# First q and k rows in 1 KB pieces on two partition halves, cast by head pairs, in a fused window attention and mixture of experts

## The chip, the cores and the metric

The kernel runs on one core of a Trainium2 chip. The time is device time of one execution in microseconds (us), as the median of several executions. A core has five engines that matter here. TensorE multiplies matrices and is written PE in the profile; loading its weights, which runs beside the multiplying, is written PEld. VectorE is DVE, ScalarE is ACT, GpSimd is POOL, and SyncE is SP. SP and ACT start transfers on hardware queues (q1 and q10 in the profile), POOL on a software queue (q0). [...]

## The reference: what is computed

Two stages, in float32. First comes attention with a window and sinks, over 4 batches, 8 heads, 768 positions and 64 dimensions per head:

```
scores = q @ k.T / sqrt(D)
keep   = (key position < 4) | ((0 <= query - key) & (query - key < 128))
a      = softmax(where(keep, scores, -1e9));  out = a @ v
```

The heads of a position are then laid side by side, which gives x with 3072 rows (tokens) of 512. Second comes a mixture of four experts with all of them used:

```
p   = domain_probs / (domain_probs.sum(-1) + 1e-9)
out = sum over e of  p[:, e] * (relu(x @ w1[e]) @ w2[e])      # w1: 512x1024, w2: 1024x512
```

## The kernel before

**Tiling.** Tokens are handled in groups of 256 (`G`): three groups in each of the four batches. Within a group, attention goes by head pairs (`hp`, four of them), since two heads of 64 dimensions fill the 128 partitions. For each pair and group it computes scores (line 676), their exponential on ACT (line 702), a mask, the product with v (lines 736 and 743), and the division by the sum (lines 770 to 782). The result is turned so that the 512 features lie on partitions (`xT`). The mixture then takes a group and an expert as a unit: first product and relu (line 1051 in the plain form, lines 1138 to 1206 in a Strassen form with seven products instead of eight), second product (line 1388 plain, line 1312 Strassen).

**Order of the work.** All engines get their instructions in a fixed order, written by a planner that runs in Python while the kernel is built. It keeps a clock for each engine and queue (`t`), estimates when each transfer has landed (`lands`, line 183, with the constants `t["sw"]`, `ROW` and `BACKLOG`), and picks the next piece of work for PE by readiness and rank (`LOW_PRODUCT`, `DUE`, `OPEN` and so on). Work for DVE and ACT waits in a list and is given out by due time (`later`, `flush`). `WIDE` is how many units of the first product may be open at once, `MIX` how many units of batch 0 may be left when batch 1 begins, `PAIR` the first batch in which two head pairs' scores may be issued together, `BACKLOG` an allowance on the landing of everything behind the first weights. When the planner sees PE with nothing ready it inserts products on zeros (`idle_products`, line 546); nine of these stand at the very start. The planner's estimates set only the order: at run time an engine waits at an instruction until its inputs are there, and all that stands behind it waits too.

**The beginning.** `load_first` (line 254) brings the first 256 positions of q and k of batch 0 as float32. They come in two halves of four heads, q from SP's queue and k from ACT's queue. Each partition holds two neighbouring positions of a head, so a contiguous piece is 2 x 64 x 4 bytes = 512 bytes, and each of the four transfers covers 128 partitions. `cast_first` (line 275) makes bf16 of them, q on DVE and k on ACT, one instruction for each half; a head pair can be turned only when both casts of its half are done. `transposes` (line 556) turns a pair with four PE transposes, two of q into one PSUM tile and two of k into another, and DVE copies q and ACT copies k into `qkT`. All other rows of batch 0 come on the software queue (`load_nat`, line 230, in 256-byte pieces), in this order: v blocks 0 and 1, q and k blocks 2 and 3, v blocks 2 and 3, the two halves of expert 0's w1, its w2, q and k blocks 4 and 5, and then the other experts. Later batches' q and k are turned by transposing transfers from SP (`turn_nat`, line 241).

**Constants and sinks.** Before the first cast, DVE makes the identity in bf16, a selector `sel2`, and a triangular mask by a scan over the identity (line 499). The identity comes from two selections on POOL (line 478). SP loads the value rows of the four sink positions, for all batches, with eight small transfers (line 473). When attention of batch 0 is done, SP stores the gates (`gates_by_row`, line 432) and the loads of batch 1 are put on the list.

Of the kernel before, what the change touches and what calls it, by code (L numbers as in the profile page):

```python
# [9 lines left out]
ALU = mybir.AluOpType  # L10
AX = mybir.AxisListType
# [5 lines left out]
def kernel(  # L17
# [44 lines left out]
    MIX = 5  # L62
    SHARE_OF = (1.034, 1.037, 1.072)
    LEAD = (1.026, 0.9853)
    DUE = 1.356
    LOW_PRODUCT = 2.147
    LOW_SECOND = 2.509
    HIGH_PRODUCT = -1
    EARLY = 0.1973
    MASK_SLACK = 200.0  # L70
    GATE = 2639.0
    GATE0 = 6000.0
    FORM = 1000.0
    TOKEN = 4559.0
    MARGIN = 2117.0
    HOLD = 0
    FULL = 8
    STEP0 = 0.2923
    READY = 40
    WIDE = 3  # L80
    OPEN = 2.551
    ONACT = 1
    ONE = 2
    PAIR = 0
    BEHIND = 2351.0
# [12 lines left out]
    t = {"pe": 1200.0, "act": 0.0, "dve": 0.0, "pool": 1280.0, "sp": 800.0, "sw": 4800.0, "hw": 0.0}  # L98
    ring, whole = [0.0] * 6, [False] * 6
    WARM = 6600.0  # L100
    FLIP, LATE = 103.6, 500.0
# [79 lines left out]
    ROW = {64: 12.8, 128: 22.6, 512: 79.8, 1024: 156.2}  # L181

    def lands(key, rows, cols, *deps):
        issued = pool(0, *deps, fixed=880)
        at = max(t["sw"], issued + 1500)
        t["sw"] = at + rows * ROW[cols] / 16
        landed[key] = t["sw"] + 900 + (BACKLOG if key[0] == "w1" or backed else 0.0)
        if key[0] == "w1":
            backed.append(key)
        moved.append([key, at, t["sw"], ROW[cols]])  # L190

    moved, backed = [], []
    BACKLOG = 1300.0
# [59 lines left out]

    def load_first():

        raw = {name: mo.tile([P, 2, 4, 2 * D], FP32, name=f"{name}raw", tag=f"wide{i}", bufs=1) for i, name in enumerate("qk")}
        for half in range(2):
            hs = slice(4 * half, 4 * half + 4)
            for name, src in (("q", q), ("k", k)):
                x = raw[name][:, half]  # L260
                (nc.sync if name == "q" else nc.scalar).dma_start(
                    out=x, in_=src[0, hs, 0:G, :].rearrange("h (p t) d -> p h (t d)", t=2),
                )
                nat[0, half, name, "raw"] = x
            landed["first", half] = ((4870.0, 5180.0), (7550.0, 7350.0))[half]
            t["sp"] += 530
# [4 lines left out]
    first = {name: sb.tile([P, 2, H, D], BF16, name="qkn", tag="qkn", bufs=NQB) for name in "qk"}  # L271
    qkn_free[-2:] = [1e12] * 2
    cast_at = {}

    def cast_first(half):
        hs = slice(4 * half, 4 * half + 4)

        def cast(at):
            cast_at[half] = at

        part = join(2, cast)
        for i, name in enumerate("qk"):
            def run(engine, i=i, name=name):
                copy(
                    engine, first[name][:, :, hs, :],
                    nat[0, half, name, "raw"].rearrange("p h (t d) -> p t h d", t=2),
                )
                part(clock(engine, 512))
            later(("dve", "act")[i], landed["first", half][i], 0, run)
# [137 lines left out]
    identf = scratch[:, 9 * P:10 * P]  # L427
    nc.sync.dma_start(out=dp, in_=moe_domain_probs.rearrange("(tb p) e -> tb p e", p=P))
# [42 lines left out]
    for h in range(H):  # L471
        r = 32 * (h // 2) + NSINK * (h % 2)
        nc.sync.dma_start(
            out=vsf[r:r + NSINK, :, 0:D], in_=v[:, h, 0:NSINK, :].rearrange("b j d -> j b d"),
        )
    ident = consts.tile([P, P], BF16, name="ident")
    for sgn in (1, -1):
        nc.gpsimd.affine_select(
            out=identf, in_=identf, compare_op=ALU.is_ge, fill=0.0,
            base=0, pattern=[[sgn, P]], channel_multiplier=-sgn,  # L480
        )
        pool(0, fixed=320)
# [3 lines left out]
    for tb in (2, 3):  # L486
# [6 lines left out]

    nc.vector.tensor_copy(out=ident, in_=identf)
    nc.vector.reduce_sum(
        out=sel2, in_=identf.rearrange("p (h x j) -> p h x j", h=NHP, j=NSINK)[:, :, 0:2], axis=AX.X,
    )
    own = lent[:, 4 * P:5 * P]
    nc.vector.tensor_tensor_scan(own, ident, ident, 0.0, ALU.add, ALU.max)
# [15 lines left out]
    def make_mask(i):  # L515
        def run(engine):
            x = (mask0, mask1)[i]
            nc.vector.tensor_scalar(out=x, in0=low[i], scalar1=1 / LOW, scalar2=1.0, op0=ALU.mult, op1=ALU.add)
            dve(4 * P)
            made.append(i)  # L520
        later("dve", 9500.0, 5000, run)
# [3 lines left out]
    t["dve"] = t["act"] = 4600.0  # L525
    cast_first(0)
    flush(4700.0)
    for x in vx:
        nc.vector.memset(x[:, :, D:DX], 1.0)
    t["dve"] += 240.0  # L530
# [25 lines left out]
    def transposes(b, g, hp):  # L556

        if b not in qkT:
            qkT[b] = sb.tile([P, 2, NHP, S], BF16, name="qkT", tag="qkT", bufs=1)
        ready = max(cast_at[hp // 2] if (b, g) == (0, 0) else rows_at(b, g), free_at(2 if (b, g) == (0, 0) else 1))  # L560
        slots, trs = [], []
        for i in range(2 if (b, g) == (0, 0) else 1):
            slots.append(pick())
            trs.append(bank(slots[i], [P, 2, 2, P], BF16, "tr"))
            ring[slots[i]] = 1e12
        hs = slice(2 * hp, 2 * hp + 2)
        for i in range(2):
            for tt in range(2):
                rows = first["qk"[i]][:, tt, hs] if (b, g) == (0, 0) else nat[b, 2 * g + tt][:, i, hs]
                nc.tensor.transpose(trs[i if (b, g) == (0, 0) else 0][:, i, tt], rows, ident)  # L570
        done = pe(4 * P, ready, n=4)
        dst = qkT[b][:, :, hp, g * G:(g + 1) * G]

        def copied(at):
            for slot in slots:
                take(slot, at)
            turned_at[b, g, hp] = at

        if (b, g) == (0, 0):
            part = join(2, copied)  # L580
            for i, engine in enumerate(("dve", "act")):
                def run(engine, i=i):
                    copy(engine, dst[:, i].rearrange("c (p t) -> c p t", t=2), trs[i][:, i].rearrange("c t p -> c p t"))
                    part(clock(engine, 2 * P))
                later(engine, done, 0, run)
        else:
            def run(engine):
                copy(engine, dst, trs[0].rearrange("c i t p -> c i (t p)"))
                copied(clock(engine, 4 * P))
            later("any", done, 300, run)  # L590
        if hp == NHP - 1:
            for _ in range(2):
                qkn_free.remove(1e12)
                qkn_free.append(done)
            qkn_free.sort()
# [221 lines left out]
    class Attention:  # L817
# [21 lines left out]
        def flip_ready(self):  # L839
            _, b, g, hp = self.flips[0]  # L840
            rows = cast_at.get(hp // 2, 1e12) if (b, g) == (0, 0) else rows_at(b, g)
            return max(rows, free_at(2 if (b, g) == (0, 0) else 1), scored_at.get(b - 1, 0.0))
# [68 lines left out]
    NH = 6  # L911
# [534 lines left out]
    while mix.more() or att.more():  # L1446
# [5 lines left out]
        if not att.more() and not loaded:  # L1452
            loaded = 1
            gates_by_row()
            turns += [(1, tb) for tb in range(NQB)]
# [102 lines left out]
```

## Time and profile before

| | |
|---|---|
| median of 3 runs | 362.27 us (361.88 to 362.48) |
| the profiled execution | 362.99 us, of which its span is 361.2 us |
| PE busy in the span | 351.7 us (97%) |
| DVE / ACT / POOL busy | 296.4 / 164.9 / 70.4 us |
| granted TensorE clock | full in every slice |
| software queue q0 | 17.31 MB in 77520 packets |
| hardware queue q1 | 18.75 MB in 38668 packets |
| hardware queue q10 (ACT's, used for the first k alone) | 0.52 MB in 1056 packets |

The span runs from the first instruction to the last, and the profiled execution's own time is 1.8 us longer. The page splits the span into 40 slices and gives the busy share of each engine in tenths. The chain of waits is followed back from the last instruction: at each step to what released it. A timeline row gives start, duration, engine, line, operation, output, inputs and count; in brackets stands how long the engine was idle before it and what ended that. In the table of stretches the columns after the stretch are its length and the busy time of PE, PEld, DVE, ACT and POOL with the number of instructions, the granted clock, the busy share of the 16 DMA engines (over 1 where several transfers are under way in each) and GB/s. Packets of the software queue are counted by the bytes that they write, so one of 128 bytes has read 256.

### The profile page before, as it was taken

Reading aid. Unit: us, or ns where it says so; the run is one execution under the profiler, and the core shown is the slowest. Engines: PE = TensorE matmul, PEld = TensorE weight load, DVE = VectorE, ACT = ScalarE, POOL = GpSimd, SP = SyncE. Lnnn points to the kernel's source line nnn. Section 1 sums busy time; section 2 is a strip of 40 time slices with the busy share of each in tenths; the row PEclk is TensorE's granted clock in tenths of the full one; section 3 lists DMA queues with packets and bytes.
Section 4 is the critical chain, followed back from the end, with each engine's and each line's share of the span. In section 5 each row is a group of like instructions: output and inputs, shape, how many; then the busy total and the mean of one; then the engine's idle time right before and its main releaser. Section 6 shows DMA issues by size and latency. Waiting matters only on the chain.

```text
span 361.2 us, 10566 instructions
## 1 busy us (share of the span) xinstructions
PE 351.7 (97%) x4410; PEld 296.2 (82%) x4423; DVE 296.4 (82%) x671; ACT 164.9 (46%) x419; POOL 70.4 (19%) x90
## 2 busy tenths in 40 slices
PE   8799999998999999999999999999999999999996
PEld 3485767756668868898899899899999999999985
DVE  4665999868868979789789989979999998987840
ACT  5764634557754463655464465546222223212110
POOL 8935016223500616101440000000000000000000
PEclk9999999999999999999999999999999999999999
DMA  9999999999943999917899131214113102000011
GB/s 172 182 186 201 210 209 177 149 126 184 149 92 97 146 175 152 135 49 74 128 155 174 16 104 31 55 50 62 37 25 89 31 22 85 16 29 33 0 61 58
DMA packets 117292, 37.25 MB, mean 103 GB/s; under 512 B 100613, under 2 KB 112741, under 8 KB 117245
## 3 DMA queue, kind: packets, MB, share of 16 engines
q0 software_dynamic: 77520, 17.31, 56.1%
q1 hardware_dynamic: 38668, 18.75, 26.0%
q8 instruction: 34, 0.56, 0.6%
q10 hardware_dynamic: 1056, 0.52, 0.5%
q14 instruction: 14, 0.11, 0.2%
HBM read 40.45 MB, written 6.34 MB: 130 GB/s over the span
## 4 chain that ended last, share of the span: by engine, by line
PE 72%; DMA 21%; POOL 4%; issue 1%; DVE 1%; ACT 0%; SPq 0%
PE acc L1312 31%; PE cps L1138 27%; DMA w<-in_moe_w_dram 11%; PE hps L1051 6%; DMA qkn<-in_k_dram 4%; DMA vx<-in_v_dram 3%; PE acc L1388 3%; DMA xT<-onat 2%; PE sps L676 2%; PE od L743 2%; POOL qkn L233 1%; POOL vx L298 1%; PE od L736 1%; POOL w L311 1%; POOL w L321 0%
## 5 line engine op out<-in xcount | busy, mean ns | idle before, releaser
L1138 PEld LDWEIGHTS <-w 128*128 128x128 bf16 x1184 | 73.3, 98 | 3.7 <-issue 1.5
L1312 PEld LDWEIGHTS <-H 128*128 128x128 bf16 x600 | 56.0, 98 | 6.2 <-issue 0.6
L702 ACT ACTIVATE aT<-sps 128x512 bf16<-128x512 f32 (+1 forms) x96 | 47.4, 573 | 18.5 <-PE sps L676 18.5
L1171 DVE SCALAR_TENSOR_TENSOR H<-cps,gates 128x512 bf16<-128x512 f32 x78 | 52.9, 682 | 1.3 <-PE cps L1138 0.2
L1138 PEld LDWEIGHTS <-vf 128*128 128x128 bf16 x768 | 47.3, 98 | 1.7 <-issue 0.4
L1312 PE MATMUL acc<-w,H 128*128 128x256 bf16 x360 | 47.7, 273 | 0.0
L1138 PE MATMUL cps<-T,w 128*128 128x128 bf16 x592 | 45.1, 219 | 0.1
L1138 PE MATMUL cps<-xT,w 128*128 128x128 bf16 x592 | 44.8, 219 | 0.0
L1388 PE MATMUL acc<-w,H 128*128 128x512 bf16 x179 | 43.4, 379 | 1.0 <-issue 0.5
L782 ACT ACTIVATE onat<-od,R 128x64 bf16<-128x64 f32 x144 | 32.9, 324 | 23.9 <-DVE R L770 23.9
L1051 PE MATMUL hps<-xT,w 128*128 128x256 bf16 x352 | 43.5, 273 | 0.1
L1184 ACT COPY cps<-cps 128x512 f32<-128x512 f32 x37 | 21.4, 579 | 38.4 <-PE cps L1138 32.8
L1138 PE MATMUL cps<-T,vf 128*128 128x128 bf16 x512 | 38.3, 219 | 0.1
L1051 PEld LDWEIGHTS <-w 128*128 128x128 bf16 x352 | 32.9, 98 | 5.6 <-issue 1.3
L1388 PEld LDWEIGHTS <-H 128*128 128x128 bf16 x192 | 17.8, 98 | 17.9 <-issue 0.3
L298 POOL DMA_DIRECT2D vx<-in_v_dram x24 | 21.4, 901 | 48.8 <-PE od L743 44.8
L1312 PEld LDWEIGHTS <-S 128*128 128x128 bf16 x288 | 27.2, 98 | 2.9 <-issue 0.2
L1191 DVE TENSOR_TENSOR cps<-H,cps 128x512 f32<-128x512 f32 x31 | 21.4, 692 | 8.4 <-PE cps L1138 5.5
L1360 ACT COPY osb<-acc 128x256 f32<-128x256 f32 x28 | 10.5, 373 | 38.3 <-PE acc L1312 38.3
L1312 PE MATMUL acc<-wf,H 128*128 128x256 bf16 x184 | 25.8, 273 | 0.0
L695 DVE TENSOR_TENSOR aT<-aT,mask 128x1024 bf16<-128x1024 bf16 (+1 forms) x36 | 22.8, 640 | 1.9 <-ACT aT L702 1.7
L1206 DVE TENSOR_TENSOR H<-H,cps 128x512 f32<-128x512 f32 x31 | 21.2, 683 | 3.8 <-PE cps L1138 3.7
(126 smaller groups left out, 543.9 us busy)
## 6 DMA issues: line engine op xcount, KB each, us to landing
w<-in_moe_w_dram POOLq DMA_DIRECT2D x7, 1024.0 KB, 16.2
out_dram<-osb SPq DMA_DIRECT2D x19, 256.0 KB
gates<-gate_rows SPq DMA_DIRECT2D x36, 128.0 KB
vx<-in_v_dram POOLq DMA_DIRECT2D x24, 128.0 KB, 6.9
qkn<-in_q_dram POOLq DMA_DIRECT2D x22, 128.0 KB, 6.8
qkn<-in_k_dram POOLq DMA_DIRECT2D x22, 128.0 KB, 7.2
w<-in_moe_w_dram POOLq DMA_DIRECT2D x2, 512.0 KB, 9.0
out_dram<-osl SPq DMA_DIRECT2D x4, 256.0 KB
```

Of the source, the lines that this page charges most:

```text
L298: nc.gpsimd.dma_start(out=vx[tb][:, :, 0:D], in_=v[b, :, tb * P:(tb + 1) * P, :].rearrange("h p d -> p h d"),)
L695: nc.vector.tensor_mul(a, a, m[:, None, :].to_broadcast([P, 2, w]))
L702: nc.scalar.activation(out=a[:, ph], in_=sps[ph][:, 0:w], func=AF.Exp, scale=scale)
L782: nc.scalar.mul(o[:, qi, hp, ph * D:(ph + 1) * D], od[:, qi, ph, 0:D], R[:, qi, ph])
L1051: nc.tensor.matmul(h[:, i].rearrange("p (q n) -> p q n", q=2), lhsT=w1_sb[e][:, db, fb * P:(fb + 1) * P], rhs=xT[b, g][:, :, db], start=(i ...
L1138: nc.tensor.matmul(y[:, f], lhsT=A[:, d, f * P:(f + 1) * P], rhs=T[:, d], start=(m in ("P1", "P5") and f == 0 and d == 0), stop=(d == 1), ...
L1171: nc.vector.scalar_tensor_tensor(out=dst, in0=src, scalar=0.0, in1=gate, op0=ALU.max, op1=ALU.mult)
L1184: nc.scalar.copy(out=tiles["Y"], in_=y)
L1191: nc.vector.tensor_add(tiles["V"], c5, tiles["X"])
L1206: nc.vector.tensor_add(c5, c5, y)
L1312: nc.tensor.matmul(x, lhsT=self.operand(b, g, e, m)[:, f], rhs=forms[e][m][:, f], start=(k == 0 and f == 0 and m in (("P1", "P5", "P2") if ...
L1388: nc.tensor.matmul(op, lhsT=H[:, fb // QF, fb % QF, s], rhs=w2_sb[e][:, fb, :], start=(fb == 0), stop=(fb == NFB - 1),)
```

## The change

1. `load_first`: still four transfers, two halves of four heads, q from SP and k from ACT. But a partition now holds four neighbouring positions (pieces of 1 KB), q lies on partitions 0 to 63 and k on 64 to 127, and q and k of a half share one tile.
2. `cast_first`: still four casts of 512 columns, but one for each head pair, with q and k together: pairs 0 and 2 on DVE, 1 and 3 on ACT. The planner's landing times for the halves become 4.4 and 5.4 us. The bf16 rows lie in one of the six `H` buffers, no longer in two of the `qkn` buffers.
3. `transposes` for the first group: each of the four turns 128 rows that hold 64 of q and 64 of k. The copies to `qkT` write every second pair of positions for both q and k, one on DVE and one on ACT.
4. Constants: the triangular mask is the result of the first selection on POOL, cast on DVE; the scan is gone. `sel2` is made behind the casts.
5. Sink rows: eight small transfers for batch 0 at the start as before, with a quarter of the rows; eight more for the other batches when attention of batch 0 is done.
6. The planner's constants have other values, so the order of instructions on all engines can differ from the start to the end.

```diff
-    MIX = 5
-    SHARE_OF = (1.034, 1.037, 1.072)
-    LEAD = (1.026, 0.9853)
+    MIX = 6
+    SHARE_OF = (1.032, 1.04, 1.072)
+    LEAD = (1.016, 0.9678)
...
-    LOW_SECOND = 2.509
+    LOW_SECOND = 1.819
...
-    GATE = 2639.0
-    GATE0 = 6000.0
-    FORM = 1000.0
-    TOKEN = 4559.0
-    MARGIN = 2117.0
+    GATE = 1837.0
+    GATE0 = 3923.0
+    FORM = 1962.0
+    TOKEN = 4373.0
+    MARGIN = 2902.0
...
-    STEP0 = 0.2923
+    STEP0 = 0.0
     READY = 40
-    WIDE = 3
-    OPEN = 2.551
+    WIDE = 2
+    OPEN = 2.423
...
-    PAIR = 0
+    PAIR = 1
...
-    t = {"pe": 1200.0, "act": 0.0, "dve": 0.0, "pool": 1280.0, "sp": 800.0, "sw": 4800.0, "hw": 0.0}
+    t = {"pe": 1200.0, "act": 0.0, "dve": 0.0, "pool": 1280.0, "sp": 800.0, "sw": 5000.0, "hw": 0.0}
...
-    FLIP, LATE = 103.6, 500.0
+    FLIP, LATE = 544.5, 604.7
...
-    BACKLOG = 1300.0
+    BACKLOG = 800.0
...
+    def new_rows(g):
+        x = mo.tile([P, H * 4 * D], BF16, name="rows", tag="H", bufs=NH)
+        nat[0, g] = x.rearrange("p (n t h d) -> p n t h d", n=NHP, t=4, h=2) if g == 0 else x.rearrange("p (h c) -> p h c", h=H)
...
     def load_first():
-        raw = {name: mo.tile([P, 2, 4, 2 * D], FP32, name=f"{name}raw", tag=f"wide{i}", bufs=1) for i, name in enumerate("qk")}
         for half in range(2):
             hs = slice(4 * half, 4 * half + 4)
-            for name, src in (("q", q), ("k", k)):
-                x = raw[name][:, half]
-                (nc.sync if name == "q" else nc.scalar).dma_start(
-                    out=x, in_=src[0, hs, 0:G, :].rearrange("h (p t) d -> p h (t d)", t=2),
-                )
+            raw.append(mo.tile([P, 4, 4 * D], FP32, name=f"raw{half}", tag=f"wide{half}", bufs=1))
+            for i, src in enumerate((q, k)):
+                (nc.scalar if i else nc.sync).dma_start(
+                    out=raw[half][64 * i:64 * i + 64], in_=src[0, hs, 0:G, :].rearrange("h (p t) d -> p h (t d)", t=4),
+                )
-            landed["first", half] = ((4870.0, 5180.0), (7550.0, 7350.0))[half]
+            landed["first", half] = (4400.0, 5400.0)[half]
...
     def cast_first(half):
-        for i, name in enumerate("qk"):
-            def run(engine, i=i, name=name):
+        for i, engine in enumerate(("dve", "act")):
+            def run(engine, i=i):
+                hs = slice(2 * i, 2 * i + 2)
                 copy(
-                    engine, first[name][:, :, hs, :],
-                    nat[0, half, name, "raw"].rearrange("p h (t d) -> p t h d", t=2),
+                    engine, nat[0, 0][:, 2 * half + i], raw[half][:, hs].rearrange("p h (t d) -> p t h d", t=4),
                 )
...
+    def load_sinks(bs):
+        for h in range(H):
+            r = 32 * (h // 2) + NSINK * (h % 2)
+            nc.sync.dma_start(
+                out=vsf[r:r + NSINK, bs, 0:D], in_=v[bs, h, 0:NSINK, :].rearrange("b j d -> j b d"),
+            )
+            sp(takes=60)
+    load_sinks(slice(0, 1))
...
-            out=identf, in_=identf, compare_op=ALU.is_ge, fill=0.0,
+            out=tri if sgn > 0 else identf, in_=identf if sgn > 0 else tri, compare_op=ALU.is_ge, fill=0.0,
...
-    nc.vector.tensor_tensor_scan(own, ident, ident, 0.0, ALU.add, ALU.max)
+    nc.vector.tensor_copy(out=own, in_=tri)
...
-                rows = first["qk"[i]][:, tt, hs] if (b, g) == (0, 0) else nat[b, 2 * g + tt][:, i, hs]
-                nc.tensor.transpose(trs[i if (b, g) == (0, 0) else 0][:, i, tt], rows, ident)
+        for x in range(4):
+            if g == 0:
+                nc.tensor.transpose(
+                    trs[x // 2][:, x % 2].rearrange("c i p -> c (i p)"), nat[b, g][:, hp, x].rearrange("p h d -> p (h d)"), ident,
+                )
...
-                    copy(engine, dst[:, i].rearrange("c (p t) -> c p t", t=2), trs[i][:, i].rearrange("c t p -> c p t"))
+                    copy(engine, dst4[:, :, :, 2 * i:2 * i + 2], trs[i].rearrange("c t i p -> c i p t"))
...
             gates_by_row()
+            load_sinks(slice(1, B))
```

## The prediction

> **What bounds the kernel now.** I read the page first, then the busy time by stretches, then the chain of waits, then the beginning in the timeline and the transfers.
>
> From the page (engine, busy us, share; then busy tenths in 40 slices of 9 us):
>
> ```profile
> span 361.2 us, 10566 instructions
> ...
> PE 351.7 (97%) x4410; PEld 296.2 (82%) x4423; DVE 296.4 (82%) x671; ACT 164.9 (46%) x419; POOL 70.4 (19%) x90
> ...
> PE   8799999998999999999999999999999999999996
> ...
> PE 72%; DMA 21%; POOL 4%; issue 1%; DVE 1%; ACT 0%; SPq 0%
> ```
>
> TensorE bounds the kernel, its clock is never held back, and the chain that ended last lies on it for 72%. So time can come only from where PE has nothing useful to do. The stretches say where (length, then busy PE, PEld, DVE, ACT, POOL):
>
> ```profile
> 0.00:5.00 5.00, 3.60 (x9) 1.34 (x10) 2.80 (x22) 2.00 (x3) 3.99 (x10) 1.00 0.55 156
> ...
> 20.00:80.00 60.00, 59.39 (x621) 42.48 (x627) 47.79 (x103) 30.27 (x62) 20.65 (x24) 1.00 1.64 179
> 80.00:90.00 10.00, 8.90 (x103) 6.08 (x103) 8.32 (x17) 7.08 (x24) 2.60 (x4) 1.00 1.38 181
> 90.00:120.00 30.00, 29.84 (x361) 22.27 (x363) 22.12 (x46) 18.30 (x55) 8.37 (x11) 1.00 1.02 117
> 120.00:130.00 10.00, 9.16 (x110) 7.01 (x109) 7.95 (x21) 4.58 (x10) 5.04 (x6) 1.00 2.38 153
> 130.00:210.00 80.00, 79.93 (x1033) 70.01 (x1030) 71.86 (x166) 41.53 (x121) 16.32 (x19) 1.00 0.99 113
> 210.00:358.00 148.00, 148.00 (x2030) 138.91 (x2027) 125.70 (x267) 49.01 (x121) 0.00 (x0) 1.00 0.17 45
> ```
>
> Between 20 and 358 us PE idles 0.61 + 1.10 + 0.16 + 0.84 + 0.07 + 0 = 2.8 us in all, most of it at 80 to 90 and 120 to 130. What is left lies before 20 us. The chain of waits runs there through POOL's loads from 1.80 us and then through the weights' transfers, so the software queue sets the pace. The timeline of the beginning (start, duration):
>
> ```profile
> 1.75 1.92 POOL L298 DMA_DIRECT2D vx<-in_v_dram  x2
> ...
> 5.13 0.62 ACT L269 CAST qkn<-kraw 128x512 bf16<-128x512 f32 x1 [1.16 <-DMA kraw<-in_k_dram]
> ...
> 6.07 0.68 PE L570 MATMUL tr<-ident,qkn 128*128 128x128 bf16 x8
> ...
> 13.73 0.90 PE L570 MATMUL tr<-ident,qkn 128*128 128x128 bf16 x13 [1.15 <-DMA qkn<-in_k_dram]
> ...
> 17.33 0.39 PE L549 MATMUL acc<-lent 128*128 128x256 bf16 x2
> 17.79 0.23 PE L736 MATMUL od<-vsd,sinkA 128*128 128x130 bf16 x1
> ...
> 18.52 1.04 PE L1051 MATMUL hps<-xT,w 128*128 128x256 bf16 x8
> ```
>
> PE waits for group 1's k until 13.73, and fills with zeros as late as 17.33. From 17.79 it runs on without a hole. The transfers show why k is late. GB/s from 0 to 30 us in slices of 0.75 us, and packets, MB and share by queue from 3 to 6 us:
>
> ```profile
> GB/s 0 0 63 100 328 345 298 297 170 154 153 156 154 154 155 152 155 176 196 209 202 205 209 216 201 206 213 205 206 210 190 171 156 155 155 171 146 179 198 211
> ...
> q10 hardware_dynamic: 1025, 0.51, 64.0%
> q1 hardware_dynamic: 842, 0.44, 52.2%
> q0 software_dynamic: 34, 0.00, 2.3%
> ```
>
> Until 6 us the hardware queues carry the raw q and k, at about 317 GB/s from 3 us on. The software queue has sent 34 packets by then and none before 5.7 us, though POOL issued its first load at 1.75. Where the engines are quieter, POOL's load of 139.58 us has its first packets between 141.1 and 141.5, so about 1.6 us after issue. At the start it takes 4 us. I read this as the software queue standing behind the raw rows.
>
> **The change part by part.** I work in the profiled execution's own time, 362.99 us (span 361.2 and 1.8 around it). It lies 0.72 above the median of 362.27; the sum is a difference, and I set it against the median.
>
> *Raw rows in 1 KB pieces.* It is the same 1.05 MB in half as many pieces. In 1.5 to 3 us the trace has 238 packets (0.12 MB) at a share of a third of the engines, so something other than the engines limits it, most simply the making of descriptors. From 3 us on the rate is 317 GB/s in 512-byte pieces. Stores in 2 KB pieces reach 393 GB/s in a slice at 340 to 350 us, and I take 355 for 1 KB, halfway. If the ramp is limited in packets it carries 0.24 MB by 3 us, and the remaining 0.80 MB take 2.27 us instead of 0.93 / 0.317 = 2.93: the end is 0.65 earlier. At 393 it is 0.9 earlier, and with a ramp limited in bytes and the old rate 0. I take 0.85, since the ramp's low share of the engines speaks for a limit in packets and the rate only refines it. If the software queue follows the raw rows, all its landings move by as much: k of group 1, then w1. The engines' share stays at 1.2 or more in the stretches from 5 to 80 us, so the queue never runs empty and the shift holds to the wait at 80 to 90 us, and PE comes there earlier by as much. Taken: -0.85. Ends: 0, and -2.4, the whole delay of 4 less 1.6. That the halves could make it later is rival C.
>
> *Casts by pairs.* Four casts before and after, 512 columns each, by rows of 0.44 on DVE and 0.62 on ACT. The first turning at 6.07 waits for ACT's cast, which ends at 5.75. After, pair 0 needs DVE's cast alone, but both q and k of the half, at 4.4 to 4.8. The nine products on zeros hold PE to 5.24, so it begins 0.8 earlier at best. On the path: 0, because PE waits 1.15 us ahead of 13.73 for group 1. If that cover were gone, up to 0.8 would show.
>
> *The hole before 17.79.* With group 0 done sooner, its last turn and product (14.47 to 14.93 in the timeline) leave the stretch after k's landing. Expert 0's first half of w1 was issued at 9.03 and takes 8.1 us to land, at 17.1; PE touches it at 18.52. After the shift it is there at 16.3, and a plan that allows 0.5 less for it (`BACKLOG`) can put a piece of 0.87 us into the fillers' place. ACT's exponentials (four in 2.06, four in 2.12 us from 15.39) still set when the values come. Taken: -0.35. Ends: 0 (the hole only moves) and -0.65 (16.46 to 17.1 filled).
>
> *Scores one by one in batch 0.* A pair issued together takes 0.55 us (33.66, 36.27), singly 0.33 each. Batch 0 has four such pairs; two lie in ACT's shadow at 15 to 17 us, two in full PE work. 2 x 0.11 = +0.2, ends 0 and +0.45.
>
> *Sink rows.* Eight transfers stay at the start (SP from 2.42 to 8.16), each with a quarter of the rows; nobody waits for them before POOL's product at 14.25. Eight more go to SP behind the gates' stores, which end at 45.9. At 0.72 us each, they hold SP to 51.6. Behind them stands the first turning transfer at 57.17, which waits for its rows. Zero, with 5.5 us of cover; without it, up to 5.7 in batch 1's turning. Their first reader runs at 74.5.
>
> *Constants.* A scan of 0.42 on DVE goes, a cast of 0.23 comes, `sel2` (0.18) moves behind the first casts. DVE idles 0.86 ahead of its first cast, and `sel2` is read at 14.25. POOL's two selections (0.29 each) stay ahead of its loads. The rows in an `H` buffer are free by about 10 us, and six such buffers wait unused until 18.5. Zero for all; without DVE's idle time 0.2 at most.
>
> *Order after 20 us.* The work is the same, seven products where there were seven. All that a better order could win is the 2.8 us of idle above. What a worse one costs, no row shows; the nearest are the two stalls of 1.1 and 0.84, and another such pair is +1.9. I take 0 and keep -1.5 (the two stalls, mostly) and +2.
>
> Sum: -0.85 - 0.35 + 0.2 = -1.0, so 362.0 for an execution like the profiled one and 361.3 against the median.
>
> **The rivals.** A is the sum above: 361.3, own range 360.5 to 361.9.
>
> B: the software queue's late start has a cause of its own (its first descriptors, its set-up). Then k still lands at 13.7 and w1 at 17.1, group 0's gain disappears in the wait at 13.73, and -0.2 for the hole and +0.2 for the scores cancel: 362.3. For it: a queue's first use can differ from later ones, and the trace has only one. Against it: the queue begins within 0.5 us of the raw rows' end. [...]
>
> C, on the slower side: the two halves of the partitions do not fill at the same time, so the raw rows come at half the rate. From 3 us, 0.80 to 0.93 MB at 355 / 2 = 178 GB/s take 4.5 to 5.2 us and end at 7.5 to 8.2, where they ended at about 6.0. Everything on the software queue moves back by 1.5 to 2.2. With +0.2 for the scores and no hole filled, that is 364.2. It decides from the point where the raw rows end after 6.2. For it: no large transfer in this trace covers only half of the partitions, so nothing shows that it is harmless. Against it: the q and the k transfers sit on two queues that ran side by side from 3 to 6 us (52% and 64%). [...]
>
> D, also slower: the new order opens a stall after 20 us, for instance with two open units instead of three. -1.0 + 2 gives 363.3. For it: one order is fixed for 4410 matmuls, and PE has no slack from 130 on. Against: from 210 to 358 us PE is full, with DVE at 85%.
>
> E: the new order also closes the stalls of 80 to 90 and 120 to 130 us: -1.0 - 1.5 gives 359.8.
>
> **How the numbers follow.** A 0.45, B 0.17, C 0.13, D 0.13, E 0.12. The prediction is A's, 361.3. Within 0.2% (0.72 us) of 362.27 is about what a measurement of this kernel cannot tell from no change, so faster means below 361.55. Faster: 0.38 of A, all of E and 0.03 of B, 0.53. Same: 0.07 of A, 0.12 of B, 0.02 of D, 0.21. Slower: 0.02 of B, C and 0.11 of D, 0.26. The range goes from E's 359.8 down to 359.6, and up to 363.9, which holds D and the milder part of C; about 0.08 of C, 0.06 of E and some of D stay outside. A's own range stands above, as cases of both signs hold much of the chance.
>
> **What would show it.** Right: the last raw packets before 5.4 us, the software queue's first near 4.9, group 1's turning released by k near 12.9, the first piece of w1's product near 17, and PE idle after 20 us still near 2.8. Wrong: the first software packet still at 5.7 (B); GB/s near 178 in the raw rows' slices and their end past 6.2 (C); PE below full anywhere after 130 us, or more than 1.1 idle in 80 to 90 (D).

## The result and the profile after

The changed kernel takes 365.14 us (median of 4 executions, 364.48 to 365.36), the kernel before 362.24 beside it. The ratio is 1.0078, with a 95% interval of 1.006 to 1.0095: slower by 2.9 us. The prediction was 361.3 with a range up to 363.9, so it had the wrong sign, and the result lies outside the range. The profiled execution took 365.35 us (before 362.99). One execution of 368.84 us, of the kernel with ten products on zeros below, was far longer than its five others and is left out of its median.

From the page of the kernel after: its span, the granted TensorE clock in 40 slices, and the chain of waits by engine.

```profile
span 363.6 us, 10602 instructions
...
PEclk9699999999999999999999999999999999999999
...
PE 93%; DMA 4%; DVE 2%; issue 0%; ACT 0%; SPq 0%; DVEq 0%
```

The span is 2.4 longer; the medians differ by 2.9, because the profiled execution of the kernel before lay 0.75 above its median. The second slice (9 to 18 us) has a 6 in the clock row, where the kernel before had nines throughout. The chain now lies on PE for 93% instead of 72%, and on DMA for 4% instead of 21%: behind its start, PE waits for little.

The stretches of the kernel after (length, then busy PE, PEld, DVE, ACT and POOL, granted clock, share of the DMA engines, GB/s):

```profile
5.00:10.00 5.00, 2.04 (x17) 1.12 (x16) 2.75 (x17) 1.91 (x5) 4.06 (x6) 0.89 2.01 182
10.00:14.00 4.00, 4.00 (x29) 1.45 (x28) 0.74 (x4) 2.67 (x7) 3.62 (x5) 0.50 3.02 147
...
20.00:80.00 60.00, 59.20 (x628) 42.62 (x635) 47.94 (x107) 31.19 (x62) 20.66 (x24) 1.00 1.59 184
80.00:90.00 10.00, 9.95 (x120) 7.14 (x119) 7.00 (x16) 7.07 (x23) 0.00 (x0) 1.00 1.53 178
90.00:120.00 30.00, 29.84 (x373) 22.79 (x374) 25.20 (x52) 20.99 (x61) 8.43 (x10) 1.00 1.03 94
120.00:130.00 10.00, 10.00 (x124) 7.83 (x123) 6.85 (x17) 5.88 (x17) 7.87 (x9) 1.00 1.33 179
130.00:210.00 80.00, 79.31 (x1017) 68.90 (x1015) 71.13 (x165) 40.27 (x117) 15.93 (x19) 1.00 1.09 118
```

Two things changed, with opposite signs. Behind 20 us PE idles 0.80 + 0.05 + 0.16 + 0 + 0.69 = 1.70 us (from 210 to 358 nothing) where it idled 2.78: the stalls at 80 to 90 and 120 to 130 are gone. In the beginning PE lost far more. From 5 to 10 us it works 2.04 of 5 us, and from 10 to 14 it is full at half the clock, with 29 matmuls where 37 ran in 2.72 us before. These stretches, two casts and a pair of bias products in the kernel before:

```profile
5.00:10.00 5.00, 4.26 (x42) 2.48 (x40) 1.86 (x7) 3.70 (x10) 5.00 (x7) 1.00 2.16 185
10.00:14.00 4.00, 2.72 (x37) 1.50 (x36) 2.70 (x10) 2.11 (x5) 3.60 (x7) 1.00 2.34 162
...
4.67 0.43 DVE L269 CAST qkn<-qraw 128x512 bf16<-128x512 f32 x1 [0.86 <-DMA qraw<-in_q_dram]
...
7.12 0.46 DVE L269 CAST qkn<-qraw 128x512 bf16<-128x512 f32 x1
...
7.39 0.50 PE L670 MATMUL sps<-lent,ident 128*128 128x384 bf16 x2
```

The timeline of the beginning after (start, duration):

```profile
5.93 0.61 DVE L284 CAST rows<-raw 128x512 bf16<-128x512 f32 x1 [3.39 <-DMA raw<-in_q_dram]
6.60 0.62 PE L582 MATMUL tr<-ident,rows 128*128 128x128 bf16 x8 [1.18 <-DVE rows L284]
...
8.45 0.62 ACT L284 CAST rows<-raw 128x512 bf16<-128x512 f32 x1 [1.92 <-DMA raw<-in_q_dram]
...
9.22 0.61 PE L582 MATMUL tr<-ident,rows 128*128 128x128 bf16 x4 [1.78 <-DVE rows L284]
9.62 0.85 PE L687 MATMUL sps<-lent,ident 128*128 128x384 bf16 x2
...
22.18 1.04 PE L1067 MATMUL hps<-xT,w 128*128 128x256 bf16 x8
```

The first cast starts at 5.93 (before: 4.67), the second half's casts at 8.45 (before: 7.12 and 7.23). PE waits 1.18 and 1.78 us for them. The two bias products at 9.62 take 0.85 us at a granted clock of 0.50 (stretch 9.62 to 10.47 us); the same two took 0.50 us before, at 1.00. The first piece of w1's product starts at 22.18 instead of 18.52.

The account closes to 0.2: the start is 3.66 later, the idle time behind it 1.08 shorter, together +2.58, against +2.4 in the span. What lies between, span less start less idle time, is 339.7 after and 339.9 before. So the loss lies in the start, and the new order gave part of it back. The experiment with the old loading, below, shows the same on an equal order.

The transfers after: GB/s from 0 to 30 us in slices of 0.75 us, then packets, MB and share by queue from 3 to 6 us, then the same from 6 to 7.5 us.

```profile
GB/s 0 0 0 93 285 277 205 229 229 180 157 145 153 142 150 150 146 141 156 186 204 206 208 206 209 199 208 228 194 205 210 208 186 164 154 155 155 154 175 174
...
q10 hardware_dynamic: 468, 0.45, 65.2%
q1 hardware_dynamic: 306, 0.30, 44.7%
...
q1 hardware_dynamic: 251, 0.25, 84.4%
```

From 3 us on the raw rows come at 205 to 285 GB/s, where they came at 297 to 345, although the pieces are twice as long. From 6 to 7.5 us a quarter of a megabyte of q is still under way. The last raw packet is at 7.31 us (before 6.25), the software queue's first at 6.84 (before 5.78): both 1.06 later. The four raw transfers land at 4.65 (k), 5.83 (q), 7.03 (k) and 8.37 (q), one after another at steps of 1.2 to 1.3 us; before they landed at 4.65, 5.11, 6.27 and 7.21.

### The profile page after: what moved, and what is told of

Its sections match the earlier page's. It is cut to its first block, busy times and chain, and to the rows that moved or that the text cites. A ratio compares the mean times of both kernels' runs of the same rounds, so it can differ in the third digit from the quotient of the medians.

```text
span 363.6 us, 10602 instructions
## 1 busy us (share of the span) xinstructions
PE 354.1 (97%) x4423; PEld 298.3 (82%) x4436; DVE 295.5 (81%) x669; ACT 166.0 (46%) x421; POOL 70.2 (19%) x90
## 4 chain that ended last, share of the span: by engine, by line
PE 93%; DMA 4%; DVE 2%; issue 0%; ACT 0%; SPq 0%; DVEq 0%
PE cps L1154 31%; PE acc L1328 30%; PE acc L1404 11%; PE hps L1067 9%; PE sps L693 3%; PE od L760 3%; DMA xT<-onat 2%; DMA raw<-in_q_dram 2%; PE od L753 1%; PE acc L562 1%; PE sps L687 1%; PE tr L586 0%; DVE onat L790 0%; PE tx L818 0%; PE sinks L654 0%; DVE aT L728 0%
## 5 line engine op out<-in xcount | busy, mean ns | idle before, releaser
L233 POOL DMA_DIRECT2D qkn<-in_q_dram x22 | 19.6, 891 | 34.5 <-DMA qkT<-qkn 27.7
```

Of the source, the lines that this page charges most:

```text
L233: nc.gpsimd.dma_start(out=both[:, i], in_=src[b, :, tb * P:(tb + 1) * P, :].rearrange("h p d -> p h d"),)
```

## The experiments

All medians with the ratio to the kernel before in the same session (before 362.07 to 362.58):

| kernel | median us | ratio, 95% interval | last raw packet | first software packet | w1's first piece | PE idle 20 to 210 |
|---|---|---|---|---|---|---|
| before | 362.24 | | 6.25 | 5.78 | 18.52 | 2.78 |
| after | 365.14 | 1.0078 (1.006 to 1.0095) | 7.31 | 6.84 | 22.18 | 1.70 |
| after, old loading | 361.28 | 0.9976 (0.9965 to 0.9987) | 6.17 | 5.77 | 18.45 | 1.18 |
| before, new loading | 362.88 | 1.0022 (1.001 to 1.0033) | 7.35 | 6.40 | 19.38 | 3.7 |
| after, ten products on zeros | 364.07 | 1.0053 (1.0035 to 1.007) | 7.26 | 6.78 | 19.98 | 2.87 |
| after, true landing times | 365.4 | 1.0088 (1.0072 to 1.0104) | 7.32 | 6.63 | 17.97 | 2.7 |
| old loading, half the raw rows | 360.97 | 0.9966 (0.9951 to 0.998) | 4.31 | 4.12 | 16.95 | 1.05 |
| full rows, two groups outermost | 395.15 | 1.09 (1.0875 to 1.0926) | 30.39 | 3.49 | 42.94 | 15.5 |
| full rows, positions outermost | 371.7 | 1.0229 (1.0203 to 1.0255) | 9.06 | 4.13 | 22.09 | 5.2 |

The last four columns are of the profiled executions, in us; a packet is counted at its start, and from 210 us on PE has no idle time to its end in any of them. In three rows the profiled execution took clearly longer than the median beside it, so the idle time is an upper reading: 362.99 for the kernel before, 364.51 for the kernel before with the new loading, and 366.9 for the one with true landing times.

**The kernel after with the old loading.** Everything new (constants, sink rows, order), but `load_first`, `cast_first` and `transposes` of the first group as before.

```diff
     def load_first():
...
-                (nc.scalar if i else nc.sync).dma_start(
-                    out=raw[half][64 * i:64 * i + 64], in_=src[0, hs, 0:G, :].rearrange("h (p t) d -> p h (t d)", t=4),
...
+                (nc.sync if name == "q" else nc.scalar).dma_start(
+                    out=x, in_=src[0, hs, 0:G, :].rearrange("h (p t) d -> p h (t d)", t=2),
...
-            landed["first", half] = (4400.0, 5400.0)[half]
+            landed["first", half] = ((4870.0, 5180.0), (7550.0, 7350.0))[half]
...
```

> The changed kernel with the old loads, casts and turning of the first group (512-byte pieces on 128 partitions); order constants, sink rows and mask as changed. Theory (the loads are the cause): raw rows end near 6.2, the software queue begins near 5.8, the clock holds, 361.0 to 362.3. Rival (the new order or its constants cost it): 364 to 365.3.

Measured: 361.28 us, faster than before by 0.24%, with an interval that lies wholly below 1. It is faster than both kernels. The last raw packet, the software queue and the first piece of w1 are back at the old times (6.17, 5.77, 18.45). Its stretches at the two old stalls:

```profile
80.00:90.00 10.00, 9.95 (x107) 6.46 (x107) 8.13 (x17) 7.25 (x24) 0.00 (x0) 1.00 1.33 183
...
120.00:130.00 10.00, 9.83 (x116) 7.56 (x114) 8.13 (x19) 6.93 (x19) 6.12 (x7) 1.00 1.85 168
```

PE had 8.90 and 9.16 there in the kernel before. So the constants, sink rows and order together are worth -0.96 us, and the new loading on top of them, with its casts, its turning and its landing estimates, costs 365.14 - 361.28 = +3.9 us. On PE, 4358 of the 4423 matmuls of the two kernels follow in the same order. Matched one by one, those of the kernel after start 3.70 us later at 20 us and still 3.70 later at 126, then 4.22 later from 127 us to the end. So on an equal order almost the whole difference is made in the first 20 us.

**The kernel before with the new loading.** The same exchange the other way, with the old landing times for the two halves.

```diff
     def load_first():
...
-                (nc.sync if name == "q" else nc.scalar).dma_start(
-                    out=x, in_=src[0, hs, 0:G, :].rearrange("h (p t) d -> p h (t d)", t=2),
...
+                (nc.scalar if i else nc.sync).dma_start(
+                    out=raw[half][64 * i:64 * i + 64], in_=src[0, hs, 0:G, :].rearrange("h (p t) d -> p h (t d)", t=4),
...
-            landed["first", half] = ((4870.0, 5180.0), (7550.0, 7350.0))[half]
+            landed["first", half] = (5180.0, 7550.0)[half]
```

> The kernel before with only the new loads, casts and turning of the first group; landing estimates 5.18 and 7.55 us, so that the order stays that of before but for the changed instructions. Theory: raw rows end near 7.2, software queue begins near 6.8, all its landings 0.5 to 1.1 later, time 363.0 to 363.8 if fillers hold the clock and 365 if it falls. Rival (the new order is the cause, the loads are harmless or good): 361.3 to 362.4.

Measured: 362.88, +0.64 us, just below the range expected. The raw rows end as late as in the kernel after (7.35), and w1's first piece comes at 19.38, only 0.86 later than before. The granted clock stays full in the profiled execution (mean 1.0). So the same loading costs 0.6 on one order and 3.9 on the other: the rows' lateness alone does not explain the result.

**The loads by themselves.** A kernel that only brings q and k (1,048,576 bytes, four transfers on the same two queues) in several forms, one after another, and reads a little of them on DVE. It leaves out all the computation and writes zeros.

```diff
+                if parts == "all" and form == "p512":
...
+                    eng.dma_start(out=dst, in_=rows(src, hs, form))
+                elif parts == "all":
...
+                    x = src[0, 2 * half:2 * half + 2, 0:2 * G, :].rearrange("h (p t) d -> p h (t d)", t=4)
+                    eng.dma_start(out=dst, in_=x)
+                else:
+                    lo = 64 * i if parts == "halves" else 0
...
+                    dst = raw[lo:lo + 64, at:at + 1024]
...
+    plan = [("p512", "all"), ("h1024", "halves"), ("h1024", "all"), ("h512", "halves"), ("h1024", "lower")]
```

> Leaves the whole computation out and writes zeros; it only times loads of 1 MB of q and k from SP and ACT, two transfers of 256 KB on each, in five forms, each form three times, one after another: 512-byte pieces on 128 partitions; 1 KB pieces with q on partitions 0 to 63 and k on 64 to 127; 1 KB pieces on 128 partitions; 512-byte pieces on the two halves; 1 KB pieces of both on partitions 0 to 63. Then the first three again with a load from POOL's queue issued beside them. If the halves are the cause: forms 1 and 3 at 300 to 370 GB/s, forms 2 and 4 at 190 to 250, form 5 no faster than 2. If the size of the pieces is: forms 2, 3 and 5 alike and 1 and 4 alike. If the software queue stands behind the hardware queues: its first packet comes when their last is out, in all three forms; if not, 1.6 us after its issue.

The timeline of DVE in this kernel, one round; in brackets how long the copy stood waiting for the last of the rows. In order: 512-byte pieces on 128 partitions, 1 KB on two halves, 1 KB on 128 partitions, and 1 KB on the lower half alone.

```profile
85.25 0.17 DVE L76 COPY got<-raw 128x8 f32<-128x8 f32 x1 [5.94 <-DMA raw<-in_k_dram]
...
101.48 0.17 DVE L76 COPY got<-raw 128x8 f32<-128x8 f32 x1 [7.27 <-DMA raw<-in_k_dram]
...
115.53 0.17 DVE L76 COPY got<-raw 128x8 f32<-128x8 f32 x1 [5.09 <-DMA raw<-in_k_dram]
...
148.60 0.17 DVE L76 COPY got<-raw 64x16 f32<-64x16 f32 x1 [7.63 <-DMA raw<-in_k_dram]
```

The other rounds give 5.93, then 7.32 and 7.30, 5.12 and 5.12, 7.79 and 7.56; in six later ones, made for POOL's queue, the first three forms give 6.41 and 6.00, 7.15 and 7.50, 5.13 and 5.18. So 1 KB pieces on all partitions are 0.83 us faster than 512-byte ones, and on two halves 1.36 us slower. The forms fall as expected if the halves are the cause, though the 512-byte rate lies below the 300 GB/s expected. Two halves together are hardly better than one half alone: from the first packet to the last, 211 to 217 GB/s on the two halves and 195 to 204 on the lower half, against 253 to 256 (512 bytes) and 311 to 314 (1 KB) on 128 partitions. A form meant to put 512-byte pieces on halves, where they lie side by side, came in packets of 1 KB as well (1077 for 1.04 MB) and with the same wait (7.15 and 7.30).

The six loads on POOL's queue were meant to run beside the rows. Five did not: POOL issued them more than 8 us ahead of the rows (242.78 against 251.29, for one), and their first packets came 1.6 us after issue. The first one was issued at 1.24, beside 512-byte rows whose packets run from 1.86 to 6.03, and its first packet came at 5.49, 4.2 us after issue. That is one case of the software queue standing behind the rows, and it is also the queue's first use in this kernel, so the runs below have to decide.

**Ten products on zeros.** The kernel after, with ten idle products of 512 columns right behind the second head pair's turns, which the planner's clock does not count. All else on PE stands in the same order.

```diff
                 nc.tensor.transpose(trs[0][:, x // 2, x % 2], nat[b, 2 * g + x % 2][:, x // 2, 2 * hp:2 * hp + 2], ident)
+        if (b, g, hp) == (0, 0, 1):
+            for _ in range(10):
+                nc.tensor.matmul(acc[1], lhsT=zeros[:, 0:P], rhs=zeros, start=True, stop=True)
         done = pe(4 * P, ready, n=4)
```

> The changed kernel with ten products on zeros (512 columns each) behind the first two pairs' turning; the planner does not know of them, so the order of all else is the changed kernel's. In the changed kernel PE idles from 7.4 to 9.2 us, the granted clock falls to half at 8.86 and comes back at 15.69. Theory (the first rows come late, and the wait also costs the clock): the clock stays full, the raw rows and the software queue are as late as before, the first piece of w1's product comes at about 19.5 instead of 22.2, time 362.5 to 363.5. If the half clock costs nothing because PE waits for data anyway: first piece at 22, 365.1. If the late rows cost nothing but the clock: at or below 362.3.

First the granted clock of the kernel after, in stretches of 3.41 us that end where it changes (length, busy PE, clock, DMA share, GB/s):

```profile
5.45:8.86 3.41, 0.84 (x10) 1.00 1.92 186
8.86:12.27 3.41, 3.05 (x17) 0.50 2.80 149
12.27:15.69 3.42, 3.42 (x33) 0.50 2.41 167
15.69:19.10 3.41, 3.41 (x49) 1.00 1.24 207
```

And the first of these stretches in the kernel with the ten products:

```profile
5.37:8.78 3.41, 2.23 (x17) 1.00 1.80 191
```

With PE busy for 0.84 of 3.41 us the clock falls to half and stays there for 6.83 us, though PE is busy 3.05 of 3.41 us and then all the time. With 2.23 of 3.41 it does not fall. The rows come as late as in the kernel after (7.26, there 7.31), and w1's first piece starts 2.20 earlier, at 19.98. That is the price of the half clock at this place. The remaining 1.53 against the old loading's 18.45 is the lateness of the rows, with whatever the other form of the casts and turns costs; the two were not taken apart.

At the end less is left: 364.07, above the range expected, so 1.07 less than the kernel after in the medians, with intervals that overlap, and 0.9 in the spans. Instruction by instruction the kernel runs 2.2 ahead of the kernel after from 17 to 131 us, and 1.04 ahead behind that. The timeline at that place:

```profile
128.83 0.29 DVE L1126 TENSOR_TENSOR T<-xT 128x256 bf16<-128x256 bf16 x1 [2.40 <-DMA xT<-onat]
...
130.38 0.35 PE L763 MATMUL od<-vx,aT 128*128 128x65 bf16 x6 [1.80 <-DVE aT L715]
```

DVE stands 2.40 us at a sum over a turned xT that has not landed, the mask stands behind it on DVE, and PE waits 1.80 for the mask. What comes earlier there meets a transposing transfer, and gives half of its lead back.

**True landing times for the planner.** The kernel after, with 5.9 and 8.4 us instead of 4.4 and 5.4 for the two halves.

```diff
-            landed["first", half] = (4400.0, 5400.0)[half]
+            landed["first", half] = (5900.0, 8400.0)[half]
```

> The changed kernel with one line other: the planner is told that the halves land at 5.9 and 8.4 us, as measured, instead of 4.4 and 5.4. Raw rows, software queue and PE's work stay as late as in the changed kernel; the planner now puts products on zeros into the wait, so the clock should hold; the order differs from the changed kernel's in some 1400 of 8867 rows on PE, all in the first third. Theory (late rows are the root, and the clock and the wrong estimates add to it): first piece of w1's product at 19 to 20, time 363 to 364.3. If the wrong estimates alone were the cause: 361.3 to 362. If neither clock nor estimates count: 365.

Measured: 365.4 us, above the range expected and no better than the kernel after. The start is mended: the clock holds from 6.71 to 88.63 us and w1's first piece is at 17.97 (not quite comparable, since PE's order differs in some 1400 instructions of its first third). But in the profiled execution the order that follows has a new stall. The stretches of PE there, and the wait that belongs to it (total, times, longest):

```profile
85.22:88.63 3.41, 1.41 (x24) 1.00 1.69 166
88.63:92.04 3.41, 3.41 (x12) 0.50 1.10 165
```

```profile
PE sinks L654 <- DMA qkT<-qkn: 2.0, 1, 2.0
```

PE waits 2.0 us for a transposing transfer, is busy 1.41 of 3.41 us, and the clock falls for one more such stretch. By these rows that is an estimated 2.0 + 1.7 us. But this execution took 366.9 us. The other four took 365.18 to 365.81 with a mean granted clock of 1.0, so they had no such fall of the clock, and without it they still were as slow as the kernel after. What makes them slow is open. The run shows that true estimates alone gained nothing with this order; whether a new search of the order on top of them would gain was not tried.

**Half of the raw rows.** The old loading on the new order, without the second half's transfers; the second casts read the first half again, so heads 4 to 7 of the first group are computed from other rows.

```diff
-                x = raw[name][:, half]
-                (nc.sync if name == "q" else nc.scalar).dma_start(
+                x = raw[name][:, 0]
+                if half == 0:
+                    (nc.sync if name == "q" else nc.scalar).dma_start(
```

> The changed kernel with the old loads (as in the run with the old loads, 361.28 us), but heads 4 to 7 of the first group are not loaded: the casts of the second half read the first half's rows. Order unchanged. It asks whether the software queue stands behind the raw rows, and what that is worth. Theory: the raw rows end near 4.2, the software queue's first packet comes at 4.0 to 4.6 instead of 5.77, k of group 1 lands 1.2 to 1.8 earlier than 12.91, time 360.0 to 361.0. Rival (the software queue's late start has its own cause): first packet at 5.7, 361.3.

Measured: 360.97, against 361.28 with all rows and inside the range expected. The raw rows end 1.9 earlier (4.31) and the software queue starts 1.65 earlier (4.12), so it does stand behind the raw rows, and its late start is not a cost of its first use. w1's first piece comes 1.49 earlier. Of this, 1.05 is left from 20 us on and 0.38 behind 127 us: the second part of the lead is eaten where DVE waits for a turned xT again (PE busy 9.22 of 10 us from 120 to 130, with all rows 9.83).

**Full rows of 1 KB.** The kernel after, with the loading in another shape and an order that the planner makes anew for it: eight transfers of 128 partitions each, in which a partition holds four positions and two groups of heads share the partitions; the pairs are turned two at a time. First with the two head groups as the outermost count, then with the 64 positions outermost.

```diff
-                    out=raw[half][64 * i:64 * i + 64], in_=src[0, hs, 0:G, :].rearrange("h (p t) d -> p h (t d)", t=4),
...
+                        out=raw[name][:, m, h],
+                        in_=src[0].rearrange("(f h) s d -> h f s d", f=2)[2 * m + h, :, 0:G, :].rearrange("f (p t) d -> f p (t d)", t=4),
...
+                        in_=src[0, :, 0:G, :].rearrange("(f h) (p t) d -> h p f (t d)", f=2, t=4)[2 * m + h],
```

> The changed kernel with its load in another shape: 1 KB pieces as in the change, but every transfer covers 128 partitions (heads 0 to 3 on the lower half, 4 to 7 on the upper, one head of each at a time, eight transfers of 128 KB), q and k in separate tiles; a step turns pairs m and m + 2 together. Theory (1 KB pieces are good, transfers to half of the partitions are bad): raw rows end at 5.3 to 5.6 instead of 7.3, the software queue begins near 5.0, k of group 1 lands near 12.3. The order of everything differs, so the time is less sure: 360 to 362. If the halves had nothing to do with it, the raw rows end at 7 again and the time is over 363.

> As the run with whole-width 1 KB pieces, but the two head groups alternate from partition to partition (position first, group second), so that the outermost step of a transfer counts 64 and not 2. If the earlier 395 us came from a transfer being given to two of the 16 engines only, because its outermost step counted 2, the raw rows now end at 5.3 to 5.9 us, the software queue begins near 5.2 and the time is 360.3 to 362.5 (the order differs from the run with the old loads, 361.28 us, in some 3700 of 8867 rows on PE). If it came from the number or size of the transfers, the raw rows are as late as 12 us or later again.

Both miss. The GB/s of the first form from 0 to 30 us, in slices of 0.75 us:

```profile
GB/s 0 0 0 34 48 134 120 171 178 169 154 173 170 173 160 61 39 41 39 40 39 49 98 205 223 219 56 39 40 95 42 60 120 219 225 186 39 39 35 34
```

Where the software queue is almost idle, the raw rows come at 39 to 41 GB/s. From 12 to 15 us the packets of the two hardware queues take 6.8% and 5.2% of the engines' time, together about two of the 16 DMA engines, and the outermost count of these transfers is 2. The first cast starts at 14.91 us and the last at 30.90 (before: 4.67 and 7.23). With 64 outermost the rows come at 259 and 232 GB/s in the slices from 2.25 to 3.75 us, with the engines busy for at least 0.8 and 0.9 of the time. But the software queue starts at 4.13, in a slice in which only 115 GB/s come (3.75 to 4.5 us), and runs beside the rows from then on: the raw rows end at 9.06, and the time is 371.7. Two things add to it: the trace's record of a full clock begins only at 14.01 us, and PE idles 4.4 us between 130 and 210 us in its new order. So this run does not settle what full rows of 1 KB are worth in the kernel. In the first form the software queue starts at 3.49, 1.74 us after its issue. So its late start at 5.8 in the kernel before is no property of the queue. It starts early in three runs: with half the rows (4.12), with about two engines in use (3.49), and with eight transfers of 64 outermost (4.13), where no run shows what lets it in.

## Why the prediction was wrong

**The step that failed: "Raw rows in 1 KB pieces", taken as -0.85.** It counted packets and left out which partitions they go to. The premise behind it, that longer pieces come faster, holds: 5.94 to 5.09 us by itself. That this is just the 0.85 that was taken is luck, since the working gave 0.65 at the rate it took, 355 GB/s, and 0.9 only at 393. The working also had 0.24 MB by 3 us, from a limit in packets at the beginning; 0.07 MB came on the two halves (68 packets from 1.5 to 3 us), and no run shows what limits the beginning; the making of descriptors was a guess. The premise that the software queue follows the raw rows holds too (5.78 to 6.84 with the rows at 6.25 to 7.31, and 4.12 with the rows at 4.31). But on two halves of the partitions the rows end 1.06 us later, not 0.85 earlier. In the loads by themselves half the partitions take in about 200 GB/s, and both halves together 211 to 217.

**The rival that held: C, "the two halves of the partitions do not fill at the same time", with a chance of 0.13.** Of its signs the main one came: the rows end past 6.2 (at 7.31; C had 7.5 to 8.2). Its 178 GB/s did not: the slices show 205 to 285. That the halves hardly fill at the same time is what these runs show: 211 to 217 GB/s on both halves together against 195 to 204 on one alone, and four transfers that land at steps of 1.2 to 1.3 us. The argument that I set against it was worth nothing: q and k "ran side by side" at 52% and 64% of the engines. After, the two queues show 45% and 65%, and the transfers still end one after another. The share of a queue counts the time for which its packets are open, and a packet can be open for longer without moving more: in the loads by themselves a packet of 1 KB is open for 72 to 75 ns (median) on the two halves and for 46 ns on 128 partitions.

C's price of 364.2 was near the result for reasons that it did not have. It had the software queue back by 1.5 to 2.2, and 0.2 for the scores; the queue went back by 1.06, k of group 1 landed 0.4 later (13.69 to 14.08) and w1's first half 0.7 (17.16 to 17.88).

**The term that no case had: the clock.** The prediction read that the clock "is never held back" and kept it so. It was not full even before: the page's row shows nines from the first slice on, but the trace's record of a full clock begins at 6.20 us (5.37 with the ten products). In the run with the ten products, the nine products on zeros ahead of that record start 0.43 us apart, and the ten behind it 0.22, so by its pace the start runs at half the clock; in the kernels before and after they start 0.43 us apart too. When the rows come late, PE has only 0.84 us of work in 3.41, since the planner believed in rows at 4.4 and 5.4 us and put almost nothing on zeros there. The half clock costs 2.2 of the 3.7 us by which w1's first piece is later than with the old loading, and the rows with their casts 1.5. At the end of the kernel, filling the gap is worth only 1.07.

**"Order after 20 us", taken as 0: low.** The new order closes the two stalls, as rival E had it (-1.5; measured -1.08 in PE's idle time in the kernel after, and -0.96 in the median of the kernel with the old loading, which has the constants and sink rows too). It had a chance of 0.12, and without the new loading the kernel would have been faster. Rival D, a new stall, did not come in the kernel after; the order made with true landing times had one of 2.0 us in its profiled execution.

**"The hole before 17.79", taken as -0.35.** With the old loading and the new plan w1's first piece stands at 18.45 instead of 18.52. That is a gain of 0.07, close to this step's lower end of 0.

**The shift "holds to the wait at 80 to 90 us".** In part. With rows that end 1.9 earlier, 1.05 of the 1.49 us at w1's first piece is still there at 80 to 90 us, but only 0.3 at the end, because the lead is lost at the turned xT between 120 and 131 us. By that run a gain of 0.85 at the raw rows would not have been worth 0.85.

**Terms of zero.** Constants and sink rows are in the kernel with the old loading, which is 0.96 faster, so no cost shows; neither was tried alone. Casts by pairs were priced by rows of 0.44 on DVE; after, DVE takes 0.61 and 0.70 for them, where it took 0.43 and 0.46. The scores issued singly (+0.2) were not separated from the order. The casts' cover, PE's wait for group 1's k, is gone after, since PE is behind by then.

## What to carry to other kernels

Ask of a transfer which partitions it covers before asking how long its pieces are: a longer piece on half of the partitions was slower than a shorter one on all (7.27 against 5.94 us for a megabyte), and a queue's busy share (45% and 65% here) did not tell whether two transfers really run side by side. When a load gets later, look at what PE does in the meantime, because idle time there can cost the clock: here 2.57 idle us in 3.41 were followed by a half clock that cost 2.2 us, more than the late rows and their casts (1.5); some cheap products in the gap took that price away here, though later waits gave half of the gain back. And where a planner fixes the order, a change to its inputs comes with a new order, so measure the load on the old order and the order with the old load before trusting the sum.

## What the runs showed of the hardware

- The clock fell after 0.84 us of work in 3.41 us (longest single wait 1.78), after 0.90 (the first form of full rows, 160.93 to 164.34 us; mean clock from 130 to 210 us 0.98) and after 1.41 (wait 2.0). It held with 2.23 (ten products on zeros), 2.12 (the kernel before with the new loading, 8.53 to 11.95 us) and 1.55 (ten products, 128.25 to 131.66 us, with the wait of 1.80 shown above). So the work in a stretch parts these cases, and the length of a single wait does not: with 1.78 it fell, with 1.80 it held. It stayed low for 6.83 us in the first case and 3.41 in the others, that is two such stretches and one; 3.05 us of work in 3.41 at half clock did not bring it back, 3.42 in 3.42 did.
- One megabyte from DRAM over two hardware queues: 311 to 314 GB/s in 1 KB pieces on 128 partitions, 253 to 256 in 512-byte pieces, 211 to 217 in 1 KB pieces on two halves, 195 to 204 on the lower half alone. What limits a half is not shown.
- Transfers with an outermost count of two used about two of the 16 engines (12% of their time at 40 GB/s), and the whole kernel became 9% slower.
- Open: why the transposing transfers of xT at 118 to 123 us take 6.9 to 8.6 us to land. POOL's loads for batch 2 run beside them there, but no run took these away. And how the software queue comes in beside busy hardware queues was seen only from its first packets (3.49 to 6.84 us).
